# Another stored order of issue for an attention and channel-mixing kernel on one core

## The chip, the cores and the metric

The kernel runs on one NeuronCore of a Trainium2 chip; the seven other cores are idle. The metric is the device time of one execution in microseconds, and the median over several executions is compared.

## What is computed

The input is q, k and v of 8 batches and 8 heads, 1152 positions of 64 numbers each. Queries are averaged in pairs, so 576 queries per head meet 1152 keys. The result, brought to 8 batches of 576 rows of 512 numbers, goes through a gated feed-forward step whose inputs are blends of each row with the row ahead of it.

```python
q_pool = q.reshape(B, H, S // factor, factor, D).mean(axis=3)
scores = scale * np.matmul(q_pool, k.transpose(0, 1, 3, 2))
attn = np.exp(scores - max); attn = attn / (sum + 1e-09)
x = np.matmul(attn, v)          # heads side by side: (B, 576, 512)
xk = mu_k * x + (1.0 - mu_k) * x_prev
xr = mu_r * x + (1.0 - mu_r) * x_prev
k = np.maximum(xk @ w_k, 0.0)
v = k * k @ w_v
r = 1.0 / (1.0 + np.exp(-(xr @ w_r)))
return r * v
```

## The kernel before

**Attention.** There are 64 head passes, and each is cut into 6 blocks of 96 queries: 384 blocks. A block's scores are nine TensorE (PE) matmuls of 128 keys by 96 queries into one of three score buffers in PSUM, s0, s1, s2 (L512, the high parts). VectorE (DVE) takes the maximum over the nine (L534). PE turns that maximum round with an identity matrix (L537), DVE reduces it across the keys (L545), ScalarE (ACT) writes the result into a row of the query tile (L526), and nine more matmuls add the low parts and subtract the maximum at once (L517). ACT takes the exponential into pf (L559), and GpSimd (POOL) cuts the low halves out of it (L521). In the first 60 blocks the maximum goes through a matmul of its own (L549). The products with the values are done in windows of 128 queries: per key chunk the matmuls L586, L588 and L591 into the one buffer a. After the last window of a head DVE divides by the sums (L607 to L612), and the result is turned, by PE (L637) for the first batch and by DMA transposes of st (L624) and a POOL addition (L626) after that, into xt.

**Feed-forward.** Tiles of 256 rows. DVE makes the blends (L743, L733, L751), PE does all products at one line (L784: w_k with 256 columns, w_r and w_v with 512), ACT takes relu, square, tanh and exp (L811, L813, L832 to L837), POOL splits the squares (L815), DVE gates (L839, L848), and a DMA writes the rows (L851). Each matrix is stored as a high and a low part. The weights are fetched and split in the first 150 us (DMA L663, ACT L671, L675, L688, DVE L678 and L690, POOL L696).

**Loads.** Keys kr and values vr (L444) and queries qr (L409) come by DMA two passes ahead. ACT and DVE or POOL split them (L452, L457, L411, L414, L418, L476, L479, L482); DMA transposes turn keys into ks1 (L468) and queries into qT (L434), and a DMA copies ks1 into ks2 (L471). All DMAs are issued by one queue, that of SyncE (SP), which waits in order.

**The order.** Nothing is put on an engine as the Python code runs. `Issue.add` only records each operation with its engine, an assumed duration and its dependencies. `Issue.run` then reads the string TURNS: for each engine in turn (DMA, DVE, ACT, PE, POOL) a number says which of the operations still left comes next. So the string alone fixes in which order every engine, the DMA queue among them, gets its work. `Issue.follow` gives each operation an assumed start under that order, and operations are emitted by these starts. `Issue.gaps` looks at the assumed pauses of PE in the first 150 us and fills a part of them with matmuls on zeros (fillers, L914), whose results are added to nothing. These keep PE occupied.

```python
ENGINES = ("DMA", "DVE", "ACT", "PE", "POOL")
turns = iter(zlib.decompress(base64.b85decode(turns)))
for e in ENGINES:
    left = [n for n in range(len(ops)) if eng[n] == e]
    while left:
        k = 0
        while (step := next(turns)) == 255:
            k += 255
        order.append(left.pop(k + step))
```

Of the kernel before, what the change touches and what calls it, by code (L numbers as in the profile page):

```python
# [29 lines left out]
SW = 256.0  # L30
# [25 lines left out]
    "(ss#m?0^w7$<h<1X<1%TCq1caDZ?;rv`Y%l!ACdg+L-_;mSZYG2d`(Dfr#lEcnm+H8)VzMrWpo$O(lic6f%f3lqls&nHn3ZflBSAQbVcKTp3@fHdm=!p)%Fg"
    "mFkLh#d@lvd{L<{mWmz4oRXzXE|bgVaI8<~>+@8gd=|yIY$B0PB$9<>HlJ<H<r3K{N)o9=GL@u6W?nXfTdG-k7sV5?csvuIl+I*g=}bDEj>Te$SRO?!X;d6d"
    "H>N3-PDLV#NF)}C_ViJAPfxg8A<ygZytXza*h0;&+oS}j+NLzMP^DUIYN95yTyAKz3xy(_Dwm8Rm5O?OJ=NDyU7?&#=X0r4sy>YqD&zs>bS9>zwWJyjhqXuq"
    "9Z!wu>oA2w3I&7QRSvg&$g&i)Xdpo7Bd6>*x^C%aK{o<A7X)yQh6Z+YM+X`X!80aWTT?wX?1nWp;Nh&@G@X`~7UWbkZdqw;Y-m8cSE-56*5$^6nMZ5Z<?9Ol"
    "g+g9ai&=CQdzqtJJ0=tPL?V~S5T#RTHL0nZu37D_tLZ8M*9yas3a+kC)@{c|w_BDjJ%eAe042I_Ii1gsvoQoM4anC}71=8MHsN^~t_RT?0X5)a)LCk)V>LHd"  # L60
    "t5tTsv5^7OP;G$caGe@Wor;vrqSte|TyHK{QoFKhx<F{(Y$lV<Fe=z68_%%kDbybCifd|Ai>R&}!YDz@hA5Qx20Tv#hnR{1jKk>57WNw*?i+!XE*Ij3{C6Xu"
    "+m<iF-f5Z_#O4N2I9D4`C!3Q@b%Huxb=3a;CH?&d_4cYg<7n(yxZXiM-R-arn9*S<S__6od(*_Wqubglt!<T-N~O|NsnEd~BrT1qp@CJ<X$_jH0#rZ|fSb*x"
    "GgO$HD&+HdN+y%(Bp}9_+@xGCpW|^LyDycX1fexlHI>rC30()`DGHE<TqO{76$*ujyx^eXGSDzw8BvqljkY#jZ_%4|9gb8gbFsAoMXfC}TcvkR6`-fFu~}7{"
    "nsoIrOM`a}C7`DsJ%SD)%G9L?3I!z(>}OLM_6$QbnZziA&B|o_&dDbe33vyiG=^R(1@~fVG-aeTJ8p1SX#p6i0Y^bohd_WqFSsBWJPfa(kS=?}Fvc4F{d!;D"
    "(mtGZ>tn`rb#?W3QD1K_TDqrOQw>#XZ-%K=z1pOjt!2Hr*;9L~O>h}JQ|C8pp`hn-MMbTz17qcL+^XEH)XB}7%i+Zm*-S&W=6WIvoQ;FyHLu~f5s4tCcrn$a"
    "uo?=7bcI}(0cBf?hj6oq+c@B3%OAT2yUo_y*UKeix&RO4RaMtR9o!9CYb)?x(VKYe>J4V83G`W36tzTD-<s7jq@*$_kQssQ67Vp~%{l61GSS9JfT!s=tQe<Q"
    "o*Ou7L=uJrDCpoHCE$7N6}K@drePq0asnR6Z(r~W%x`RL#H0>0RD{hS;*|kX0L>dJ6aDDm*AWd##kt|?4rmGkR>4igo1)-Uk+%;_8Gy|kIDCL}Q>LP10L7Cg"
    "j-No|$0=i}U+wQxdbP0_Bwf8dy*)h>y2f{Rb#W)F7)zaMXNS_>+ScFJ*4ozEN-dLHIwo{tXtgM9Rx33%H&v0EsM=qxR%EtPQOo6VEoJ7GWz{lDnh=nx<+0VW"
    "LX|RFx75(En0a!rVOfc0&ze=7HFKt-)J><tv}y1;J1`mVFd;RGlnE2Y(YSGmcz>L_mF^yjz%8_BJ9V~_($?luOQ2Z=*H$d6vDiRXu?VE8B}E15D3{NtGg%OB"
    "5-gij6pEuq;-z>o!kKWSnZjWVP>)#Qcx=d#>jdfoj-x_kq%brT+csu^K!eO%2KUxXV+Oas!iq_OwP;jjzAuj&lS|nr)D{i~eI+W6;rCUjSgd2us2c;fUZISV"  # L70
    "CZH>gUQ3b^ZKFt}8c9c>sY0R7Pz0H<7lLc-mg{;h;-l+=SDl#S)WJms^l0*)Oq1bma0r{A%Z%QmPnAA0gEq5^RH<~r%hqyvEWE6+mjjI*lK0_Tsk=njmr4^z"
    "L2S(z3cwGru5iqj23#c+Zn|hw6rPqC@)T<g$D#^*8V+@ZlyDojDS0djov4hhwjEH&K9afIkWI*jQM=F&uJgGmHGq4PGLdNf`0?m)X%l9R<&%DpdVhaE_0df5"
    "O+QWR8-pWtc6HIru1=!%xeB#*f<38~s!CM_7^pl6FNhAP;@!&SgUiZfWQs}=dWUsSp-=}?pl%oy>2yk3mARF`luC+X7~FFbl#C}9P@J_2zc4x_Gz*08_4j*y"
    "gpoqs-Q6?0-7!kn-0rS1)TMSR9n?Ofy{(O?g{_^awY61kQJb5UGMfJYz#oI5aawr{f=@$38<l_!7}fKU>I-#EeRb?0<ypx<fc0}ElFiRP5@!>ds>Er23~r^P"
    "(PT6liLiTfBN4<K&pW{L6b4N1+}>UVE;`iJ$?eo`!Wn97X`Kn5THD|r2o!^}r3v0uX<E5U0#`O1nr)htkVSS6W2&yuz)rDiRgOE9%aHUdl>$j;%D#IFI8uqn"
    "RccH|6Le@S7H22n8;>*c!ZeQ$9)Qd+1~$kZgK#p~)um8Jhe>VSZ3L3hTP4*HRf)snMCldt2vr)(9h1sL5VfU>Y%%<Ch$*mlP*wF%vPzo!v7BmzPxZ2EnY@!k"
    "@p!$2FM9+7c#-E54^k0v8iOksz(6C3S_OkjF(uzBHHj_FA)YJ||M{k2h5@pc`B5=08A6J3Lj62IQAV1jISwW@re|`w7S=QnOEiio20@RidF+r09}NSi5cHmd"
    "X@q9-6G4<iyUOYVvMvwR7<d7Alt@^<YpUt0csLNS?Qj@xj);!;2;&Oz!{9hVH71`!hXK?M2OPYm6$n@u#HJ}d;(K`}7jvRSRx*h?Tz<r};GFcraxKs$deF8*"
    "p`@L_FTww$lkhLq-X~0Uf-eR5VaOu99@$WF(4-u@BM~Q)k-kZfLS{UUp9jNv@G^+E;?970Pk3?EfOoQkcGQjF2GklvH%9>@^6*=M5IOt^*N<5i-qYcZM#W}*"
    "ef?-7ODFg3!%=8L!^J)ONa#YRPrl$M_kQ>x_8)%o;isSO-o1D4Zrt**P-xFbAB~KBJTkIx<X<DZa2)wyWY;dDJ@hF*^f#iv@7%rn-T!&_J)*z<)yKp?-~QX*"  # L80
    "-{#C;wr$(CW5@RG+hy_J-XePE%~xc8>&q{{x)sMi(Hn0Nz4FS_Tj;45pL&X3MA_yoTYmRDdUklz@bI(4!<#oh^9(=n=u<?v;fW`Rens>cZ5SSYWW&R<vR~7q"
    "kJ3XAadzXw4{zLv;~g-%f8*^NZePEiZoBQa`yPCd?xmj-cK6}(U3cHLZk_M!9oT+CbTbVN{dnlQp|7BR<uyb<^s|>@`!3N%Yu2t^L#tP>z6jfYU2+NbbT+M#"
    "x14p>*?jocw`k?c6)RS(TuF2~&cFFhzlIa(lv9>3U&`5Kbka#*|2ol8M91N5*^(s-X~BX8#~i=lxUYRp-h4D2d+bq1&6_um=!m1}$VH0|B07)`T{O7xkV6Is"
    "al^dB52v|v{hH?xvV(&xbOsI>m@{YAEMN1`?AbGBOomOT88c|wH2?02Q>W5|2{PN+**|e&XJ4N@>B01&yPG&nRyr#^JsllPJ|IwznAAv^ILM12BYA(NQV-_K"
    "=XnPzVpR^yh>!?j{tFYf@Pro=mazEDijl+`pV!(KAjD2#K+^8dY2UujKBJF5BH-$aFFyHX7i{<EpYPrcu<a)L=+lozb_0BSMn3pN;t%#d?WFhL1Mc31{q5a<"
    "{9_b<Z|?vu-+1dSdj0jc7=?e?_WJ9iz4|h}_S&ER1em?>0&RWemCc*~@Q2Mrf8a~M|NZ98@}6ht`Qhh)HMS>f&po=~kqwV+*zgGFA0xu?m&n~u^x*nCiPkf)"
    "0HUAs<vZ7{`#CZ<aQ>(M(?1>>x^~D%*VXhNcCp;AUVZMl7hOcOibw*9&O8$kB1Y2b45V)WOJ|;W;))fteEITI=(N*LJ^@8^{3x=P0$a<LFDFJ8>{vSf_+ySa"
# [867 lines left out]
```

## Time and profile before

| | |
|---|---|
| three executions | 1104.06, 1099.98, 1105.12 us; median 1104.06 us |
| profiled execution | 1100.48 us, of it 1098.7 us from the first to the last instruction |
| busy PE, DVE, ACT, POOL | 97%, 80%, 69%, 68% of the span |
| mean granted TensorE clock | 0.998 of full speed |
| HBM | 67.11 MB read, 9.44 MB written |

A busy share counts the time in which at least one instruction of that engine runs. Matmuls overlap each other in the pipeline, so PE counts as busy also where the next matmul comes a little late; only longer pauses show as idle time. "L534" is line 534 of the kernel before; in the changed kernel every line after the table has a number larger by 2.

### The profile page before, as it was taken

Reading aid. Unit: us, or ns where it says so; the run is one execution under the profiler, and the core shown is the slowest. Engines: PE = TensorE matmul, PEld = TensorE weight load, DVE = VectorE, ACT = ScalarE, POOL = GpSimd, SP = SyncE. Lnnn points to the kernel's source line nnn. Section 1 sums busy time; section 2 is a strip of 40 time slices with the busy share of each in tenths; the row PEclk is TensorE's granted clock in tenths of the full one; section 3 lists DMA queues with packets and bytes.
Section 4 is the critical chain, followed back from the end, with each engine's and each line's share of the span. In section 5 each row is a group of like instructions: output and inputs, shape, how many; then the busy total and the mean of one; then the engine's idle time right before and its main releaser. Section 6 shows DMA issues by size and latency. Waiting matters only on the chain. (4 is left out here: it accounts for less than half of the span.)

```text
span 1098.7 us, 43186 instructions
## 1 busy us (share of the span) xinstructions
PE 1068.2 (97%) x18625; PEld 875.1 (80%) x18625; DVE 873.6 (80%) x1565; ACT 763.0 (69%) x1419; POOL 746.4 (68%) x750
## 2 busy tenths in 40 slices
...
GB/s 229 215 214 144 169 195 105 186 144 112 148 122 126 128 101 144 142 112 131 125 99 125 123 140 128 104 93 175 65 135 141 99 147 76 146 32 35 10 20 39
DMA packets 257647, 135.25 MB, mean 123 GB/s; under 512 B 192944, under 2 KB 229808, under 8 KB 257456
## 3 DMA queue, kind: packets, MB, share of 16 engines
...
q8 instruction: 145, 2.38, 0.9%
...
HBM read 67.11 MB, written 9.44 MB: 70 GB/s over the span
## 5 line engine op out<-in xcount | busy, mean ns | idle before, releaser
L521 POOL TENSOR_SCALAR pl<-pf 128x864 f16<-128x864 uint16 (+1 forms) x384 | 353.7, 921 | 190.5 <-ACT pf L559 157.9
L534 DVE TENSOR_REDUCE mx<-s 128x96 f16<-128x864 f32 x384 | 402.4, 1052 | 57.1 <-PE s L512 39.8
L559 ACT ACTIVATE pf<-s 128x864 int32<-128x864 f32 x384 | 339.9, 888 | 137.1 <-PE s L517 110.4
L586 PE MATMUL a<-vt,pf 128*128 128x65 f16 x2880 | 302.0, 193 | 4.2 <-issue 2.7
L588 PE MATMUL a<-vt,pf 128*128 128x64 f16 x2880 | 302.3, 193 | 0.0
L586 PEld LDWEIGHTS <-pf 128*128 128x128 f16 x2880 | 255.4, 98 | 9.2 <-issue 2.8
L588 PEld LDWEIGHTS <-pf 128*128 128x128 f16 x2880 | 250.5, 98 | 15.2 <-issue 2.5
L591 PE MATMUL a<-vb,pl 128*128 128x65 f16 x2304 | 254.2, 193 | 0.0
L512 PE MATMUL s<-qT,ks 128*128 128x96 f16 x3456 | 225.7, 206 | 4.2 <-ACT pf L559 2.5
L517 PE MATMUL s<-qT,ks 128*128 128x96 f16 x3456 | 223.3, 206 | 1.9 <-ACT qT L526 1.5
L591 PEld LDWEIGHTS <-pl 128*128 128x128 f16 x2304 | 212.8, 97 | 0.1
L512 PEld LDWEIGHTS <-ks 128*128 128x128 f16 x3456 | 186.6, 98 | 30.5 <-issue 5.9
L517 PEld LDWEIGHTS <-ks 128*128 128x128 f16 x3456 | 181.2, 98 | 21.8 <-issue 2.9
L526 ACT ACTIVATE qT<-s 1x96 f16<-1x96 f32 x384 | 90.4, 236 | 98.6 <-PE s L537 80.7
L545 DVE TENSOR_REDUCE mx<-s 128x1 f16<-128x128 f32 x324 | 92.9, 287 | 66.0 <-ACT qT L526 64.0
L784 PE MATMUL f<-xhk,wk_hi 128*128 128x256 f16 x496 | 135.1, 272 | 0.9 <-DVE em L848 0.7
L784 PE MATMUL f<-xlk,wk_hi 128*128 128x256 f16 x496 | 135.1, 272 | 0.2 <-DVE xlk L751 0.2
L784 PE MATMUL f<-xhk,wk_lo 128*128 128x256 f16 x496 | 135.2, 273 | 0.0
L784 PEld LDWEIGHTS <-wk_hi 128*128 128x128 f16 x1152 | 105.8, 98 | 15.1 <-issue 1.3
L815 POOL TENSOR_TENSOR gl<-g 128x512 f16<-128x512 f32 x72 | 79.0, 1104 | 39.7 <-ACT g L813 25.9
L537 PE MATMUL s<-identb,mx 128*128 128x128 f16 x384 | 84.5, 221 | 8.9 <-DVE mx L534 5.6
L784 PE MATMUL f<-wv_hi,g 128*128 128x512 f16 x240 | 90.9, 379 | 1.2 <-ACT ex L832 1.2
...
## 6 DMA issues: line engine op xcount, KB each, us to landing
...
out_dram<-em SPq DMA_DIRECT2D x36, 256.0 KB, 2.9
...
```

Source lines behind the costliest of these rows:

```text
L512: nc.tensor.matmul(cols(c, c + 1), ks1[hp][:, c, :], qhi, start=(c == c0), stop=False, skip_group_check=True)
L517: nc.tensor.matmul(cols(c, c + 1), ks2[hp][:, c, :], qlo, start=False, stop=True, skip_group_check=True)
L521: op("POOL", 0.917 if buf == ("pside",) else NC * (r1 - r0) / 1200 + 0.27, lambda: nc.gpsimd.tensor_scalar(to, half(pf, U16, 0)[:, :, HALF ...
L526: op("ACT", 0.131, lambda: nc.scalar.activation(qlo[0:1], src, AF.Prelu, scale=scale, alpha=(1.0 + EPS) / (1.0 - EPS)), r=[("s", at)] + kl ...
L534: op("DVE", 0.974, lambda: nc.vector.tensor_reduce(mxz[:, P - QN:P], grid(0, NC).rearrange("p c q -> p q c"), axis=AX.X, op=ALU.max), r=[( ...
L537: op("PE", 0.057, lambda: nc.tensor.matmul(s[:, 0:P], mxz, identb, start=False, stop=False, skip_group_check=True), r=[("mx", z), ("col", ...
L545: op("DVE", 0.199, lambda: nc.vector.tensor_reduce(to, s[:, 0:P], axis=AX.X, op=ALU.max), r=[("s", z), ("row", z)], w=[("col", z1) if join ...
L559: op("ACT", NC * QN / 1200 + 0.067, lambda: nc.scalar.activation(pf[:, :, HALF + rows.start:HALF + rows.stop], grid(0, NC), AF.Exp, bias=S ...
L586: nc.tensor.matmul(a_b[:, a0:a0 + VN], half(pf, F16, 1)[:, c, his], vt[jv][:, c, D:D + VN], start=(w == 0 and c == 0), stop=False, skip_gr ...
L588: nc.tensor.matmul(a_b[:, a0:a0 + D], half(pf, F16, 1)[:, c, his], vt[jv][:, c, 0:D], start=False, stop=(side and c == NC - 1), skip_group ...
L591: nc.tensor.matmul(a_b[:, a0:a0 + VN], pl[:, c, rows], vb[jv][:, c, 0:VN], start=False, stop=(c == NC - 1), skip_group_check=True)
L784: nc.tensor.matmul(ps, terms[i][0], terms[i][1], start=(first and i == 0), stop=(i == last), skip_group_check=True)
```

## The change

Only the string TURNS is another one, two lines longer. No operation of the kernel, no tile, no size and no dependency differs. The new string is said to come from a search that judges an order over several draws in which transfers land late or early; the old one was found with one fixed lateness. Since the fillers follow from the assumed pauses, their number changes too: 146 before, 168 now.

```diff
 TURNS = (
-    "c-nnh378bswLZ01b#?W=ch7XsbWhJd%*H-|AjpUUE`SSB&>$KmZV`mIJQs{Hnm9(IQAsrJ8YODLBrb8HPesKTh*8`yQ4?MgM{q$=3HSZyR*&Y(_r7=TRMo9p"
...
-    "T?^f<*o`LtM-!o+jgpC)(PD~RtBi#5=+IDvYKxWOP!V3o6kbvZan%a>EBTINhS0SZn}fGk%s{|2ZNsrGn-qggUDf6C<(HuLmpDe(H2xQVP3K+"
+    "c-n1x378ed+3wrR={|i<pM9CL%$eoPzA+07>#ztSOHd#nzZ>I-CSpWHL`6l>ENV1H{+JjSaES)=YGOiAqwzPRCYlJwl?08(M8{k;Dx)Ic+V}mc58mfK&#ju%"
...
+    ">(u"
 )
```

The following rows show three places. In names such as qT0 or ks1_0 the number behind the tile is the buffer; the number after the underscore only counts tiles. First, the SP queue (all DMAs) at the head of the program, before:

```order
L434 DMA_TRANSPOSE qT0_85<-qn0_69 128x4x128
L444 DMA vr0_75<-in_v_dram 128x576
L434 DMA_TRANSPOSE qT0_85<-qn0_69 128x4x128
L663 DMA st1_122<-in_moe_w_k_dram 128x1024
L471 DMA ks2_1_84<-ks1_1_82 64x1152
L663 DMA xt2_107<-in_moe_w_k_dram 128x1024 x2
L434 DMA_TRANSPOSE qT1_86<-qn0_69 128x9x128
L663 DMA st0_121<-in_moe_w_k_dram 128x1024
L434 DMA_TRANSPOSE qT1_86<-qn0_69 128x9x128
L468 DMA_TRANSPOSE ks1_0_81<-kn0_79 128x9x128
```

and now:

```order
L436 DMA_TRANSPOSE qT0_85<-qn0_69 128x4x128 x2
L665 DMA st1_122<-in_moe_w_k_dram 128x1024
L473 DMA ks2_1_84<-ks1_1_82 64x1152
L665 DMA xt2_107<-in_moe_w_k_dram 128x1024 x2
L470 DMA_TRANSPOSE ks1_0_81<-kn0_79 128x9x128
L446 DMA vr0_75<-in_v_dram 128x576
L665 DMA st0_121<-in_moe_w_k_dram 128x1024
L384 DMA mu_r_156<-in_moe_mu_r_dram 128x4x1
L436 DMA_TRANSPOSE qT1_86<-qn0_69 128x9x128
L665 DMA st1_122<-in_moe_w_k_dram 128x1024
L436 DMA_TRANSPOSE qT1_86<-qn0_69 128x9x128
```

The transpose of the third head's keys (ks1_0) moved ahead of the two transposes of the next queries (qT1); the third head's values (vr0) moved behind three fetches of weights.

Second, DVE at the head of the program, around the first maxima, before:

```order
L466 COPY ks1_0_81<-s0_131 128x512
L411 TENSOR_TENSOR qs0_78<-qr0_77 128x256
L479 SCALAR_TENSOR_TENSOR vt0_87<-vr0_75,vt0_87 128x4x64
L534 TENSOR_REDUCE mx0_96<-s0_131 128x96
L534 TENSOR_REDUCE mx1_97<-s1_132 128x96
L545 TENSOR_REDUCE mb0_99<-s0_131 128x1
L479 SCALAR_TENSOR_TENSOR vt0_87<-vr0_75,vt0_87 128x5x64
```

and now:

```order
L413 TENSOR_TENSOR qs0_78<-qr0_77 128x256
L468 COPY ks1_0_81<-s0_131 128x512
L459 TENSOR_TENSOR kn1_80<-kr1_74,kn1_80 128x9x64
L536 TENSOR_REDUCE mx0_96<-s0_131 128x96
L536 TENSOR_REDUCE mx1_97<-s1_132 128x96
L547 TENSOR_REDUCE mb0_99<-s0_131 128x1
L481 SCALAR_TENSOR_TENSOR vt0_87<-vr0_75,vt0_87 128x4x64
```

Between the copy of ks1 and the first maximum, two steps (qs and a part of vt0) gave way to one (the low part of the second head's keys, kn1); the vt0 step now stands behind the first L545.

Third, DVE around block 198, in the middle of the run, before:

```order
L534 TENSOR_REDUCE mx2_98<-s2_133 128x96
L733 SCALAR_TENSOR_TENSOR xk_108<-xr_109,mu_k_155,xt2_107 128x192
L839 SCALAR_TENSOR_TENSOR ex0_117<-ex0_117,em0_119 128x512
L545 TENSOR_REDUCE mx0_96<-s2_133 128x1
L534 TENSOR_REDUCE mx0_96<-s0_131 128x96
L733 SCALAR_TENSOR_TENSOR xk_108<-xr_109,mu_k_155,xt2_107 128x192
```

and now:

```order
L536 TENSOR_REDUCE mx2_98<-s2_133 128x96
L735 SCALAR_TENSOR_TENSOR xk_108<-xr_109,mu_k_155,xt2_107 128x192
L547 TENSOR_REDUCE mx0_96<-s2_133 128x1
L536 TENSOR_REDUCE mx0_96<-s0_131 128x96
L735 SCALAR_TENSOR_TENSOR xk_108<-xr_109,mu_k_155,xt2_107 128x192
L841 SCALAR_TENSOR_TENSOR ex0_117<-ex0_117,em0_119 128x512
```

The gate step of the feed-forward (L839, now L841) moved from ahead of a maximum to behind it.

## Rows read from the trace of the kernel before

**Rows 1.** The page: busy time by engine, and the instruction packets of PE's queue.

```profile
PE 1068.2 (97%) x18625; PEld 875.1 (80%) x18625; DVE 873.6 (80%) x1565; ACT 763.0 (69%) x1419; POOL 746.4 (68%) x750
...
q8 instruction: 145, 2.38, 0.9%
```

**Rows 2.** Busy time by stretch; columns: length, engines with counts, clock, DMA share, GB/s.

```profile
0.00:10.00 10.00, 7.36 (x95) 7.00 (x95) 7.21 (x29) 6.45 (x12) 3.36 (x11) 1.00 0.78 229
10.00:50.00 40.00, 33.24 (x677) 29.52 (x675) 34.91 (x64) 30.78 (x60) 17.11 (x20) 0.96 1.09 243
50.00:150.00 100.00, 94.12 (x2030) 84.77 (x2027) 96.73 (x169) 88.16 (x171) 72.22 (x73) 1.00 0.81 179
150.00:1000.00 850.00, 840.27 (x15164) 695.98 (x15163) 701.82 (x1240) 601.67 (x1117) 629.23 (x626) 1.00 0.59 121
1000.00:1098.70 98.70, 93.19 (x669) 57.78 (x667) 32.94 (x66) 35.90 (x64) 24.46 (x23) 1.00 0.10 26
```

**Rows 3.** Waits of PE, 150 to 1000 us: us in total, times, longest.

```profile
PE s L537 <- DVE mx L534: 4.0, 11, 1.0
PE s L537 <- DVE mx L545: 2.8, 7, 0.7
PE a L586 <- DVE xb L612: 1.1, 2, 0.7
```

**Rows 4.** Waits of PE and then of DVE, start of the run to 150 us.

```profile
PE a L586 <- issue: 2.7, 1, 2.7
...
DVE mb L545 <- PE s L537: 3.7, 2, 3.4
```

**Rows 5.** DVE in order of time, 8 to 10 us.

```profile
8.37 0.42 DVE L411 TENSOR_TENSOR qs<-qr 128x256 f32<-128x256 f32 x1
8.71 0.92 DVE L479 SCALAR_TENSOR_TENSOR vt<-vr,vt 128x256 f16<-128x256 f32 x1
9.54 2.01 DVE L534 TENSOR_REDUCE mx<-s 128x96 f16<-128x864 f32 x2
```

**Rows 6.** The fillers by line: count, busy us, mean ns of one, idle us before them.

```profile
L914 PE MATMUL a<-zero 128*128 128x128 f16 x83 | 8.6, 265 | 0.9 <-DVE zero L329 0.9
...
L914 PE MATMUL s<-zero 128*128 128x128 f16 x63 | 5.1, 221 | 0.0
```

**Rows 7.** PE in order of time, around 24 us.

```profile
23.79 0.20 PE L591 MATMUL a<-vb,pl 128*128 128x65 f16 x1
26.71 0.24 PE L586 MATMUL a<-vt,pf 128*128 128x65 f16 x1 [2.72 <-issue]
```

**Rows 8.** DMA packets by queue, 11 to 24 us, and 24 to 31 us below.

```profile
q1 hardware_dynamic: 4036, 3.31, 100.4%
q14 instruction: 1, 0.01, 0.2%
...
q8 instruction: 2, 0.03, 2.0%
```

**Rows 9.** The SP queue, then POOL, in order of time, 14 to 33 us.

```profile
14.53 0.51 SPq L444 DMA_DIRECT2D vr<-in_v_dram  x1
...
23.01 1.70 SPq L434 DMA_TRANSPOSE qT<-qn  x1
...
27.36 2.51 SPq L468 DMA_TRANSPOSE ks<-kn  x1
...
23.50 0.67 POOL L482 TENSOR_SCALAR vb<-vr 128x576 f16<-128x576 f32 x1
32.13 1.42 POOL L521 TENSOR_SCALAR pl<-pf 128x864 f16<-128x864 uint16 x2 [7.96 <-issue]
```

**Rows 10.** DVE, POOL and PE in order of time, 496 to 500 us.

```profile
497.07 1.38 DVE L839 SCALAR_TENSOR_TENSOR ex<-ex,em 128x512 f32<-128x512 f32 x1
498.38 0.28 DVE L545 TENSOR_REDUCE mx<-s 128x1 f16<-128x128 f32 x1
498.58 1.04 DVE L534 TENSOR_REDUCE mx<-s 128x96 f16<-128x864 f32 x1
...
496.03 1.89 POOL L521 TENSOR_SCALAR pl<-pf 128x864 f16<-128x864 uint16 x2 [1.36 <-ACT pf L559]
...
499.68 0.23 PE L537 MATMUL s<-identb,mx 128*128 128x128 f16 x1 [1.02 <-DVE mx L534]
```

**Rows 11.** Two DVE lines: duration in ns, min/median/max.

```profile
L839 DVE SCALAR_TENSOR_TENSOR ex<-ex,em x36: 674/693/1384, 164.1 to 1093.8; 128x512 f32<-128x512 f32 x36
...
L733 DVE SCALAR_TENSOR_TENSOR xr<-xr,mu_r,xt x96: 269/477/1661, 134.1 to 1066.5; 128x256 f32<-128x256 f32 x48, 128x64 f32<-128x64 f32 x16, 128x192 f32<-128x192 f32 x16, 128x128 f32<-128x128 f32 x16
```

**Rows 12.** The chain that ended last, its pieces off PE after 1000 us.

```profile
1010.98 0.18 SPq L851
...
1011.27 4.37 DMA st<-st
...
1094.86 0.69 DVE em L848
```

More of the change, by code (lines that the diff above doesn't have):

```diff
@@ L56 @@
[L56 to L87, printed above, removed]
@@ new lines @@
+    "(=*|!uukbiIue?lgOy7L-B2)O1#R20+;lt?3p!4)6hp`kXvi6Cj|KwJLq^uo<DrlfEb4kp<O;`v!64#xD1bydV1`mb%d%~&1imAs4p@=6WtfJOMIsms1$8$b"
+    "v~?@trh>s#F2q}TV>%e%I|SplX=Q_MFbl&r?0^B&NJpd8O@`0l$<~7j7r~Gnv%|4~MfI6ciz*HT_yCI&sO!`NG)|XB{b-y>qp_(`YiQ85`ufiL`f@$$8Yeb4"
+    "Hlw+zp%D!zm+F~oODLgOtJT!j)uINuTuUyOFEH2TP*tocq8i0~L1RNYU6oE}sx$dwzO7J5=bPD*&ZaZj4AQxy)LqSa>6J=lQt5O)Jtddtc==qisw$aGrjx}~"
+    "F4bCvT%xK9_1SDymiS6CCwkG>)7y)lD3R6~iL|$CZYx^C;U+DF=60>AwF%9&O(6>1P+u;UtZI}3g<@@eEo#l0+8UHfRg|(^EM}Ri_(H4|Q9xBrPZ*hu8H?$O"
@@ new lines @@
+    "s2Pb;ML^6c#RyQ>jkva*vJoU=Y*=B0D#>&lLd6V(@+^lO$4UAPRC35PIBCSx0?X2M-8FQgR}boTm(%5T*lcUj^`^!~k<_5tQP+$nO>|wZuCC!<X+o(KFp9-M"
+    "T_Imnqn8Ygau!giPv@x2X`;$}Do40xh=Y`2Seg-~1X@so9kgpHXCM%Q<4j~@MJOIv45}nzn`X5%srrd*BCez(1jaUOJ)lbpha(XRFVfq38(LdiS~RUmBV5dK"
+    "S+B2euBYTpgpwYp18VYSE?3Cq^Z9~-s!~-46`Uy+nhMBso(YR|COxH)My?8+R^2dDrfJ9Zcq|;&-4Gu`3$((8a99gXL`Cv|BvH2Gh?0Hj<z1>OHQQDVaEujH"
+    "x=q8e^cW3McO$xCI7b;%?E!s?%)<nIyx!kG)ZcH68)u?#0>+Q0<XwH}?PTgQI=ecJjt)a-TMIhS-q^;(S!!%<>g4fjjX+Cli{2d2DOSB+uh&8=X($%5Dxss0"
@@ new lines @@
+    ";j7Q3Rb(J9s}kX!&-YU!L_Dn^odyKydNymAx{*w#=)1z<STt;f5_(9SC^2V+!?VL-dMi2#YoOCQp+jp&dmCS~$!zpfTYKA_b{<+=Dc=x*MDVnhb)%`t(d}~C"
+    "Fzf2{LZMVD=y??K8mg+bVsTPY<|CiU&>ESDqMV<7S*K>ww9FhWnhDt~%`ufs>WOS1lhO4$%St8;U9j(ld7_aJE3WG<jkutvR|YXpX3R9lN|I^m={~NzdrbG3"
+    "F@1gL>qT!*Zx3~?cXa3h3a<w&!_pgC4Wp%5uhSc9%e8t<Z7pF?UENS!trzQ{8K9MB3Wf2-!ni^~#HOk<1*KQYpUWL49w(C)T#4jaB{vhLC5)pfJ(+|SkJIbX"
+    "mNi=?8fVyA77mMl*Fp{|sHzCwH@460?KREu-R2mev$wBT@9EJ^nz7-unXLptLqkKL+)ze+v#vEZa%gnb)tPm*rco+UB%)ssQC%%|oAX5#FPQ1zixfn~QbkP)"
```

92 lines of the change are left out of this document (57 added, 35 removed).

## Prediction

> **What bounds the kernel now.** I read the page first. PE is busy for 1068.2 of 1098.7 us, DVE for 873.6 [rows 1], so at most 30.5 us of the span show PE idle, and a mere reordering can win no more than that plus what little hides between matmuls. Next I cut the span into stages [rows 2], because the share of busy time mixes three of them.
>
> In the first 10 us PE idles for 2.64 us: data are not there yet. From 10 to 50 us PE idles for 6.76 us and from 50 to 150 us for 5.88 us, but there DVE is the bound: it works for 34.91 of 40 and 96.73 of 100 us, since it also splits the weights. What the start can give back is therefore DVE's own idle time, 5.09 and 3.27 us, together 8.4 us. From 150 to 1000 us PE idles for 9.73 us of 850, DVE for 148: PE bounds, and the waits that are left are short ones for the maxima, 4.0 us in 11 waits for L534 and 2.8 us in 7 for L545, and 1.1 us in 2 for the division of the sums [rows 3]. After 1000 us PE idles for 5.51 us. Part of that is the end: the last gate starts at 1094.86 us, and then the result is written [rows 12]; nothing in an order shortens it.
>
> So the visible stakes are 8.4 us in the start, 9.7 us in the middle, and little at the end.
>
> **The change, part by part.** All operations stay, with the fillers as the only ones that are added. Outside the three places shown, the table moves hundreds of steps by one or two places; I price the stages.
>
> *First maxima.* In the trace the first L534 starts at 9.54 us, behind the 0.92 us of a vt0 step that began at 8.71 us [rows 5]. Now that step stands behind the first L545, and the low part of kn1 stands in the place of qs and vt0. At worst this brings nothing, since the scores themselves have to be there; at best the first maximum comes 0.83 us earlier (9.54 less 8.71). I take 0.3 us, nearer to nothing: the moved step is still DVE work, and DVE is full right afterwards. Term: -0.3 us.
>
> *Fillers.* 22 more, at 94 ns each (8.6 and 5.1 us for 146 of them [rows 6]), are 2.1 us of PE time. They stand in the first 150 us, where PE has 15.3 us of idle time by the stages above and DVE sets the pace. They are hidden by that; if the cover were gone they would cost the whole 2.1 us. Term: +0.3 us.
>
> *The DMA queue in the start.* At 23.79 us PE stops for 2.72 us, and the releaser named is "issue": nothing that the trace shows held it [rows 7]. DVE then waits 3.4 us for PE, its only long wait from 10 to 150 us (two waits of this kind, 3.7 us together) [rows 4]. From 11 to 24 us the data queue has 100.4% of the engines' time and not one packet of PE's instruction queue is seen; two come in the 7 us after [rows 8], where 145 over 1098.7 us [rows 1] would make about one per 7.6 us. So I read the stop as PE out of instructions behind a crowded set of DMA engines. The Trainium skill (Runtime: NRT & Kernel Launch, Instruction fetch mechanics) says that instructions come in 16 KiB blocks by a DMA queue of the engine's own and that crossing a block's end is mostly hidden; by that rule the stop would be an accident, the new order would not have it, and the sum would be lower by 2.7 us. The rows show 2.72 us that were not hidden, so the sum goes by the rows. The new order keeps the crowd: three fetches of weights still stand one behind another there, and one transpose moves from 27.36 us to ahead of the one issued at 23.01 us [rows 9]. The stop may go (-3.4 us, DVE's wait) or come twice (+3.4 us). Between these ends I take 0, as the queue before and now holds the same transfers within a few places. The values vr0, moved behind three fetches, were issued at 14.53 us and used by POOL at 23.50 us, after which POOL stood idle for 7.96 us [rows 9]. That idle time hides a lateness of some microseconds, so I price it at nothing; without it POOL's next cuts, and the windows behind them, would wait as long as the values do, which lies inside the 3.4 us if they come by 27 us.
>
> *The middle.* Here DVE is often full only for a moment. At 497.07 us the gate L839 takes 1.38 us where its median is 0.693 us, then L545 and L534 follow, and PE waits 1.02 us at L537 [rows 10, 11]. It is a slow copy of L839 and not its place alone: until 497.92 us POOL was cutting low halves (two L521 from 496.03 us, 1.89 us together [rows 10]). In the new order L839 stands behind that maximum, so this wait should go. But the other orders of steps meet other POOL steps. To judge this I counted, for blocks 60 to 383 and with the median durations of the trace, the DVE work between two successive maxima against the PE work between the ends of their scores: DVE has more by over 0.5 us in 15 places before and in 8 now, and over all places where it has more, the excess is 19.3 us before and 17.3 us now. Ten per cent less excess on 9.73 us is 1.0 us. The ends are -9.7 us (every visible wait goes) and +9.7 us (as many again). Term: -1.0 us, close to nothing, because the count hardly moves.
>
> *The end.* One output DMA stood between two transposes of the last result, on the chain for 0.18 us [rows 12]; now it stands ahead of both. Against it, ACT now does both scalings of the last mix ahead of a tanh and an exp, which then wait for the transposes. I take 0, ends -0.2 and +0.6 us.
>
> Sum: -0.3 + 0.3 + 0 - 1.0 + 0 = -1.0 us. Against the profiled execution's own 1100.48 us that is 1099.5 us. That execution lies 3.6 us below the median of the three runs (1104.06 us), near the lowest (1099.98 us); the mean of the four is 1102.4 us. Less 1.0 us this gives 1101.4 us, and **1101 us** is my forecast.
>
> **The rivals.**
>
> *Faster.* The start loses its stop and the middle half of its waits: 3.4 + 0.5 x 9.7 = 8.3 us, thus 1102.4 - 8.3 = 1094 us. For it: the place of the wait of 1.02 us is visibly relaxed, 15 crowded places became 8, and an order that was judged against late and early transfers should depend less on one. Against it: the waits of PE in the middle name DVE and no DMA [rows 3], so what such a search guards against is not what costs time there.
>
> *Slower.* DVE steps with two inputs in SBUF fall under POOL steps more often. The place is DVE's queue from 150 to 1000 us; the price is what L733 shows, 1661 ns against 477 ns, or L839 with 1384 against 693 [rows 11]; it decides once such a step stands directly ahead of a maximum about twice as often as now. Then the visible waits double: 1102.4 + 9.7 = 1112 us. For it: hundreds of small moves draw these meetings anew, and nothing in the string knows where POOL really is. Against it: the count of crowded places did not rise. The Trainium skill (SBUF — State Buffer, Who interferes with whom) has the rule: DVE and GpSimd share one pair of ports under an exclusive lock, and the loser blocks until the other's instruction ends. The 1.38 us beside POOL's 1.89 us agree with it [rows 10].
>
> *The order changes nothing that ends last.* The fillers and the table move, but each stage is bound as before: 1102.4 us. This lies in the forecast's own range.
>
> **How the numbers follow.** About 0.5% (5.5 us of 1104.06) is what a measurement of this kernel can tell from no change; that puts "faster" below 1098.5 us and "slower" above 1109.6 us. The forecast with the case of no effect has 0.48, the faster rival 0.34, the slower one 0.18. I lean to the faster side because both counts that I could make fell. The forecast's own range, by the stop (3.4 us either way) and some of the middle, is 1097 to 1106 us. To leave out no more than 2 in 10 it has to reach towards both rivals: 1091 us takes in the faster one, 1110 us the slower one up to its last part.
>
> **What would show it.** Right: the stages 150 to 1000 us still show 8 to 11 us of PE idle time, mostly L537 waiting for DVE; DVE stays above 95% busy from 50 to 150 us; a stop of PE with releaser "issue" of 2 to 4 us somewhere before 60 us; 168 fillers, without a longer start. The wait at block 198 should be gone. The forecast is wrong if PE idles for less than 6 or more than 15 us in the middle, if DVE's idle time from 10 to 150 us leaves the band from 5 to 12 us, or if PE waits for a DMA anywhere after 150 us.

## The result and the profile after

Before: 1103.68 us, the median of four executions (1099.98 to 1105.12). After: 1090.78 us, the median of four (1087.42 to 1091.95). The ratio is 0.9883, with a 95% interval from 0.9849 to 0.9917: **faster by 12.9 us**, and 0.2 us below the low end of the predicted range. The profiled execution of the changed kernel took 1087.42 us, of it 1085.6 us from the first to the last instruction, against 1098.7 us in the one before, so 13.1 us less.

The page of the changed kernel, answering to [rows 1]:

```profile
PE 1064.7 (98%) x18647; PEld 876.1 (81%) x18647; DVE 865.6 (80%) x1565; ACT 761.7 (70%) x1419; POOL 745.3 (69%) x750
...
q8 instruction: 146, 2.39, 0.9%
```

DVE does the same 1565 instructions in 8.0 us less. Busy time by stretch, with the columns of [rows 2]:

```profile
0.00:10.00 10.00, 7.99 (x80) 7.49 (x81) 5.99 (x28) 6.15 (x11) 2.48 (x10) 1.00 0.74 223
10.00:50.00 40.00, 35.07 (x765) 31.31 (x762) 38.18 (x68) 32.75 (x64) 19.51 (x22) 1.00 1.06 231
50.00:150.00 100.00, 94.42 (x2036) 85.55 (x2033) 96.11 (x171) 88.58 (x173) 72.10 (x73) 1.00 0.81 190
150.00:1000.00 850.00, 845.54 (x15260) 700.96 (x15259) 694.47 (x1248) 604.05 (x1119) 630.26 (x627) 1.00 0.58 121
1000.00:1085.60 85.60, 81.70 (x521) 50.79 (x519) 30.89 (x54) 30.19 (x55) 20.93 (x19) 1.00 0.06 23
```

From 150 to 1000 us PE's idle time fell from 9.73 to 4.46 us. Waits of PE there, answering to [rows 3]:

```profile
PE s L539 <- DVE mx L536: 2.3, 4, 1.0
PE f L786 <- ACT ex L834: 1.2, 1, 1.2
PE s L539 <- DVE mx L547: 0.3, 1, 0.3
```

The waits for the two maxima went from 6.8 us in 18 to 2.6 us in 5. No wait for a DMA is among them. The single wait for ACT is near 997 us; the kernel before has one just like it after 1000 us, outside its stretch.

**Where in time the 13.1 us come from.** Each block has one L537 (now L539), so the same block can be found in both traces. Block 59 starts its L537 at 137.11 us before and 136.42 us after, 0.7 us earlier. From block 59 to block 383 it takes 861.1 us before and 850.3 us after, 10.8 us less; from there to the end 100.5 and 98.9 us, 1.6 us less. But PE does its matmuls in another order, so the same block is not the same amount of work done. The feed-forward products ahead of block 59's turn, before and now:

```profile
0.00:137.11 137.11, 9.77 (x72) 6.45 (x72) 0.99 0.89 194
0.00:136.42 136.42, 11.61 (x84) 7.36 (x84) 1.00 0.90 203
```

The new order has by then done 12 more of these, 9 more L512 and 5 more L517 (now L514 and L519), 1.9 us of work at the median distances of 0.109 and 0.042 us from one such matmul to the next; ahead of block 383 it has done 0.9 us more. Counted by equal work PE has gained 2.6 us by block 59, **9.9 us in the middle** and 0.7 us at the end. All differences of the middle below are counted in this way; from block to block each is 1.0 us larger.

**Idle time shows only half of it.** From 150 to 1000 us PE has 5.27 us less idle time, yet the middle is 9.9 us shorter. A matmul counts as busy to its modelled end, while the next could start much earlier (L591 and L586 follow each other at some 0.03 us and each is shown for 0.2 us). I measured each distance from one matmul's start to the next against the median distance for its kind. By that sum PE lost 18.1 us from 150 to 1000 us before and 9.9 us after. Of it 11.6 us in 31 places before, and 5.6 us in 20 after, stand directly ahead of L537, the matmul that waits for the maximum.

**What the new order does on DVE.** Its two-input steps are shorter on average. Lines of DVE from 150 to 1000 us in the kernel before (count, busy us, mean ns, idle us ahead):

```profile
L479 DVE SCALAR_TENSOR_TENSOR vt<-vr,vt 128x576 f16<-128x576 f32 x54 | 49.2, 911 | 0.4 <-ACT vt L476 0.4
L411 DVE TENSOR_TENSOR qs<-qr 128x576 f32<-128x576 f32 x26 | 26.7, 1028 | 0.0
L751 DVE SCALAR_TENSOR_TENSOR xlk<-xk,xhk 128x512 f16<-128x512 f32 x28 | 25.4, 910 | 0.9 <-ACT xhk L748 0.8
```

and in the changed kernel:

```profile
L481 DVE SCALAR_TENSOR_TENSOR vt<-vr,vt 128x576 f16<-128x576 f32 x53 | 53.1, 1003 | 0.0
L413 DVE TENSOR_TENSOR qs<-qr 128x576 f32<-128x576 f32 x26 | 24.2, 930 | 0.1
L753 DVE SCALAR_TENSOR_TENSOR xlk<-xk,xhk 128x512 f16<-128x512 f32 x29 | 20.3, 703 | 0.9 <-ACT xhk L750 0.7
```

The low parts xlk take 703 instead of 910 ns each, qs 930 instead of 1028; the values vt go the other way, 1003 instead of 911. I call **stretch** what DVE's steps take beyond the lower quartile of their own line and shape. Over 150 to 1000 us it is 51 us before and 42 us after. And in the run of DVE steps that leads up to a late maximum, the stretch is as long as the loss in 11.1 of the 11.6 us before, and in 5.0 of the 5.6 us after. Each of the 92 steps that took over 0.15 us more than their quartile before (84 after) ran while a POOL step ran. POOL runs most of the time and such a run of steps can be long, so this shows that the stretch is enough, not that it is the cause. So theory 1 was: PE waits for maxima that are late because, just ahead of them, DVE's steps stood still beside POOL's. Theory 2: DVE's work is spread better between maxima, POOL or no POOL. Theory 3: transfers.

The place around block 198 [rows 10], DVE in the changed kernel in order of time:

```profile
489.63 0.29 DVE L547 TENSOR_REDUCE mx<-s 128x1 f16<-128x128 f32 x1 [0.33 <-ACT qT L528]
489.88 1.06 DVE L536 TENSOR_REDUCE mx<-s 128x96 f16<-128x864 f32 x1
490.85 0.41 DVE L735 SCALAR_TENSOR_TENSOR xk<-xr,mu_k,xt 128x192 f32<-128x192 f32 x1
491.19 0.68 DVE L841 SCALAR_TENSOR_TENSOR ex<-ex,em 128x512 f32<-128x512 f32 x1
```

and POOL there:

```profile
486.98 4.09 POOL L523 TENSOR_SCALAR pl<-pf 128x288 f16<-128x288 uint16 x4
491.57 1.07 POOL L523 TENSOR_SCALAR pl<-pf 128x864 f16<-128x864 uint16 x1 [0.50 <-ACT pf L561]
```

The gate L841 now runs behind the maximum and begins in a gap of POOL (491.07 to 491.57 us): 0.68 us where it was 1.38 us. The wait of 1.02 us is gone.

### The profile page after: what moved, and what is told of

Read it like the earlier page. It is cut to its first block, busy times and chain, and to the rows that moved or that the text cites. A ratio compares the mean times of both kernels' runs of the same rounds, so it can differ in the third digit from the quotient of the medians.

```text
span 1085.6 us, 43226 instructions
## 1 busy us (share of the span) xinstructions
PE 1064.7 (98%) x18647; PEld 876.1 (81%) x18647; DVE 865.6 (80%) x1565; ACT 761.7 (70%) x1419; POOL 745.3 (69%) x750
## 4 chain that ended last, share of the span: by engine, by line
PE 89%; DVE 6%; ACT 2%; issue 1%; DMA 0%; ACTq 0%; DVEq 0%
PE f L786 35%; PE s L514 12%; PE s L519 12%; PE a L588 7%; PE a L590 7%; PE a L593 6%; PE s L786 5%; DVE mx L536 3%; PE s L539 2%; PE a L786 2%; ACT pf L561 1%; DVE xr L735 0%; PE s L551 0%; DVE mx L547 0%; DVE xb L614 0%
## 5 line engine op out<-in xcount | busy, mean ns | idle before, releaser
L590 PE MATMUL a<-vt,pf 128*128 128x64 f16 x2880 | 309.4, 193 | 1.4 <-issue 1.4
L588 PE MATMUL a<-vt,pf 128*128 128x65 f16 x2880 | 309.1, 193 | 0.7 <-DVE xb L614 0.3
L593 PE MATMUL a<-vb,pl 128*128 128x65 f16 x2304 | 258.3, 193 | 0.0
L514 PE MATMUL s<-qT,ks 128*128 128x96 f16 x3456 | 232.1, 206 | 4.1 <-ACT pf L561 3.4
L519 PE MATMUL s<-qT,ks 128*128 128x96 f16 x3456 | 230.5, 206 | 1.5 <-ACT qT L528 1.2
L514 PEld LDWEIGHTS <-ks 128*128 128x128 f16 x3456 | 189.6, 98 | 34.2 <-issue 6.9
L519 PEld LDWEIGHTS <-ks 128*128 128x128 f16 x3456 | 184.0, 98 | 20.4 <-issue 2.2
L786 PE MATMUL f<-wv_hi,gl 128*128 128x512 f16 x240 | 91.0, 379 | 0.0
```

Source lines behind the costliest of these rows:

```text
L514: nc.tensor.matmul(cols(c, c + 1), ks1[hp][:, c, :], qhi, start=(c == c0), stop=False, skip_group_check=True)
L519: nc.tensor.matmul(cols(c, c + 1), ks2[hp][:, c, :], qlo, start=False, stop=True, skip_group_check=True)
L588: nc.tensor.matmul(a_b[:, a0:a0 + VN], half(pf, F16, 1)[:, c, his], vt[jv][:, c, D:D + VN], start=(w == 0 and c == 0), stop=False, skip_gr ...
L590: nc.tensor.matmul(a_b[:, a0:a0 + D], half(pf, F16, 1)[:, c, his], vt[jv][:, c, 0:D], start=False, stop=(side and c == NC - 1), skip_group ...
L593: nc.tensor.matmul(a_b[:, a0:a0 + VN], pl[:, c, rows], vb[jv][:, c, 0:VN], start=False, stop=(c == NC - 1), skip_group_check=True)
L786: nc.tensor.matmul(ps, terms[i][0], terms[i][1], start=(first and i == 0), stop=(i == last), skip_group_check=True)
```

## The experiments

**One half of the order at a time.** Both strings in one kernel; every step that one order assumes to start before 150 us stands in that order, all others follow in the other.

```diff
+        first = plan(new)
+        q = {e: [n for n in new[e] if first[n] < 150.0] + [n for n in old[e] if first[n] >= 150.0] for e in ENGINES}
```

New start, old rest:

> The new order up to 150 us of its own assumed starts (on every engine and the DMA queue), the old order for all steps after that. Between the two full orders the difference is 12.9 us; by the block times in the traces about 3 us of it had come by 150 us and about 10 us came between 150 and 850 us. If the stages add up, this kernel wins the start's part alone: 1100 to 1101 us, and PE idles some 9 to 10 us from 150 to 1000 us, as before. If a better start is what makes the middle better (steps of POOL and DVE meet elsewhere because they begin elsewhere), it comes near the changed kernel, 1091 to 1095 us. If the start's part was chance, 1103 to 1105 us.

Old start, new rest (the same with the two swapped):

> The old order up to 150 us of its own assumed starts, the new order for all steps after that. If the stages add up: 1093 to 1095 us (1090.8 plus about 3), and PE idles 4 to 6 us from 150 to 1000 us. If the middle's gain hangs on the start, 1099 to 1104 us. The sum of this kernel's gain and the other hybrid's should be near 12.9 us if the parts are independent.

Measured: 1101.19 us (ratio 0.998, 0.9963 to 0.9997) and 1094.84 us (0.9915, 0.9891 to 0.994), 2.2 and 8.5 us below the kernel before; together 10.7 of 12.9 us, the rest within the intervals. PE's line for 150 to 1000 us, new start with old rest:

```profile
150.00:1000.00 850.00, 837.91 (x15108) 693.79 (x15107) 701.36 (x1235) 598.78 (x1110) 623.02 (x623) 1.00 0.59 120
```

and old start with new rest:

```profile
150.00:1000.00 850.00, 843.96 (x15250) 700.13 (x15249) 695.82 (x1239) 604.83 (x1119) 628.04 (x628) 1.00 0.60 121
```

The stages add up: about a sixth of the gain comes with the start, two thirds with the rest, whose idle time follows the new order (6.0 us) and not the new start (12.1 us).

**POOL's cut of the low halves shortened**, in both orders. The later blocks read stale low halves.

```diff
-  to, half(pf, U16, 0)[:, :, HALF + r0:HALF + r1], LO, ...
+  to[:, 0:1] if i >= 60 else to, half(pf, U16, 0)[:, 0:1 if i >= 60 else NC, HALF + r0:HALF + r1], LO, ...
```

> The old order with POOL's cut of the low halves (L521) shortened from nine key chunks to one from block 60 on, so that the low halves of the later blocks are not renewed: POOL is busy for far less, and DVE steps with two inputs in SBUF meet hardly any POOL step. Theory 1 (the middle's gain is fewer and shorter DVE steps that stand still beside a POOL step): the stretch of the DVE steps, 51 us in the trace of the kernel before from 150 to 1000 us, nearly goes, and this kernel falls by 8 to 14 us, to 1090 to 1095 us. Theory 2 (the gain is DVE work that is spread better between the maxima, by the order alone): it falls by less than 5 us, to 1099 to 1103 us. Theory 3 (transfers that come late): no change but what the cut itself held, within 3 us.

> The new order with the same shortening of POOL's cut from block 60 on. Read against the old order with the same shortening: theory 1 says the difference falls from 12.9 us to about 3 to 6 us (the start's 3 us and a rest); theory 2 and theory 3 say that it stays at 10 to 15 us. Absolutely: theory 1 gives 1085 to 1089 us, theory 2 1086 to 1090 us; the difference between the two orders decides, not this number.

Measured: 1096.97 us (0.9941, 0.9921 to 0.9961) and 1088.05 us (0.9858, 0.9832 to 0.9885). The old order fell by 6.4 us, the new one by 2.7 us; the difference shrank from 12.9 to 8.9 us. Both numbers lie between the theories. POOL was still busy for 402 us and DVE's stretch still 28 and 26 us.

**All repeated POOL steps shortened**, in both orders; keys, values, blends and squares of the middle are then stale in part as well.

```diff
-  gl[:, f2, 0:n], g32[:, f2, 0:n], gh[:, f2, 0:n]
+  gl[:, f2, 0:n // 8 if t0 else n], g32[:, f2, 0:n // 8 if t0 else n], gh[:, f2, 0:n // 8 if t0 else n]
...
```

> The old order with all of POOL's repeated steps shortened to about an eighth or less (L521 from block 60, the low parts of keys L457 and the values L482 from pass 12, L623 and L626 from the third and fifth batch, L763 and L815 from the second tile on); the skipped parts keep stale numbers. Shortening L521 alone took 6.4 us off the old order and 2.8 us off the new one, and left POOL busy for 403 us from 150 to 1000 us and DVE's stretch at 28 and 26 us. Theory 1 (meetings with POOL steps are the whole of the middle's difference): a further fall of 4 to 6 us, to 1091 to 1093 us. Theory 1 and 2 together (about half each): 1 to 3 us lower, 1094 to 1096 us. Theory 2 alone: within 1 us of 1097.

> The new order with the same shortening of all POOL steps. What decides is the difference to the old order with the same shortening, 8.9 us when only L521 was short. Theory 1: it falls to 3 to 5 us (the start's part). Both theories in halves: it stays at 6 to 9 us. Theory 2: 9 us or more. Absolutely 1086 to 1088 us by all of them.

Measured: 1090.28 us (0.9875, 0.9852 to 0.9898) and 1085.59 us (0.9836, 0.9814 to 0.9858), 4.7 us apart, and 0.7 and 0.4 us below the ranges. From block 59 to 383 the two take 848.8 and 847.9 us; by equal work they do not differ (0.1 us the other way), where the full kernels differ by 9.9. The stretch of 150 to 1000 us, old order:

```profile
150.00:1000.00 850.00, 846.39 (x15308) 703.09 (x15307) 664.87 (x1255) 605.93 (x1125) 217.15 (x629) 1.00 0.59 121
```

and new order:

```profile
150.00:1000.00 850.00, 846.81 (x15275) 702.70 (x15274) 666.69 (x1257) 603.79 (x1119) 215.66 (x627) 1.00 0.59 121
```

DVE's work takes 37 us less than in [rows 2] though none of its steps changed. With POOL nearly out of the way the old order is in the middle as good as the new one. The 4.7 us are theory 1's number, and theory 2 alone falls. But shorter POOL steps also give their results earlier, and that remained as another reading.

**POOL busy again, with steps on a scrap tile.** Behind each shortened step a contiguous POOL step on a tile that nobody reads.

```diff
+  def idle(size):
+      if size > 0:
+          nc.gpsimd.tensor_scalar(junk[:, 0:size], junk[:, 0:size].bitcast(U16), LO, 1.0, ...)
```

> The old order with all POOL steps shortened as in the two kernels that shortened them all (old order 1090.3 us, new order 1085.6 us, 4.7 us apart), and behind each shortened step a POOL step on a scrap tile that nobody reads, sized so that POOL is again busy for some 630 us from 150 to 1000 us. The results of POOL are thus early, while POOL occupies itself about as long as in the full kernel. If DVE is held by POOL being at work (meetings), the gain of the shortening goes again: 1097 to 1104 us. If what counted were POOL's results coming earlier, it stays at 1090 to 1093 us.

> The new order with the same shortened POOL steps and the same scrap steps. Meetings: 1087 to 1092 us, and 8 to 13 us below the old order in the same form. Early results: 1085 to 1087 us, and 4 to 6 us below it.

Measured: 1090.65 us (0.9889, 0.9858 to 0.992) and 1084.56 us (0.9824, 0.9803 to 0.9844), so both as without the scrap steps. Read by its expectation this would speak for early results. But its condition, POOL busy for some 630 us again, failed; old order:

```profile
150.00:1000.00 850.00, 846.58 (x15309) 702.53 (x15306) 676.61 (x1252) 605.76 (x1125) 541.85 (x1159) 1.00 0.60 121
```

POOL gained 325 us of work, and DVE's busy time only 12 us. Steps of this form, in shorter pieces, hardly hold DVE, so the run says nothing on what the real steps do.

**The same with the rest of each real step**, short step first, the rest (same operands) on a scrap tile:

> The old order with POOL's steps shortened as before, but behind each short step now stands the rest of the real step (same operands, same form, about eight ninths of the length) with its result on a scrap tile that nobody waits for. The contiguous scrap steps of the last try did not occupy DVE as the real ones do: they put POOL's busy time from 217 back to 542 us, but DVE's from 665 only to 677 us, against 702 us in the full kernel. Here DVE's busy time from 150 to 1000 us should come back to 690 to 702 us. If holding DVE (and POOL's own occupation) is what costs, the old order comes back to 1097 to 1103 us. If the early results of POOL were the gain, it stays at 1089 to 1092 us.

> The new order in the same form. Meetings with POOL's real steps: 1087 to 1091 us, and 8 to 13 us below the old order in this form. Early results: 1084 to 1087 us, and 4 to 6 us below it.

Measured: 1134.13 us (1.0265, 1.0239 to 1.0291) and 1126.66 us (1.0205, 1.0183 to 1.0227), slower than anything expected. Two steps for one overfilled POOL; waits of PE from 150 to 1000 us in the old order:

```profile
PE a L605 <- POOL pl L529: 18.3, 22, 1.7
PE a L600 <- POOL pf L529: 3.3, 4, 1.2
```

POOL itself became what PE waits for, which it is nowhere in [rows 3], and DVE's 687 us stay short of the 690 to 702 us that were the condition. Inconclusive.

**Each real POOL step whole, one for one, its result on a scrap tile.** Nobody waits for POOL's results in the middle any more; what POOL does and how long stays.

```diff
-  to, half(pf, U16, 0)[:, :, HALF + r0:HALF + r1], LO, ...
+  scrap(NC, r1 - r0) if i >= 72 else to, half(pf, U16, 0)[:, :, HALF + r0:HALF + r1], LO, ...
...
```

> The old order with every POOL step of the middle (from block 72, pass 14, the third batch, the fifth batch or the third tile on, as the buffers allow) in its full length and form, but with its result on a scrap tile, so that nobody waits for POOL and the stale numbers are read. POOL's busy time from 150 to 1000 us stays near 630 us, and it is one step in the place of one step, so POOL is not overfilled as in the last pair. If DVE being held by POOL's steps is what costs: as the full kernel, 1099 to 1104 us, with PE's losses at L537 near 11 us. If POOL's results coming late is what costs: 1089 to 1093 us.

> The new order in the same form. Meetings: 1088 to 1092 us, so 9 to 13 us below the old order in this form. Late results: 1084 to 1087 us, and 4 to 6 us below it.

Measured: 1099.84 us (0.9983, 0.9968 to 0.9998) and 1091.54 us (0.9912, 0.9895 to 0.9928), 8.3 us apart. The old order by stretch:

```profile
150.00:1000.00 850.00, 840.55 (x15175) 696.68 (x15174) 704.09 (x1240) 602.13 (x1118) 615.16 (x626) 1.00 0.59 121
```

and its waits of PE there:

```profile
PE s L541 <- DVE mx L538: 3.1, 8, 1.1
PE s L541 <- DVE mx L549: 2.8, 7, 1.2
```

DVE is back at 704 us, the waits for the maxima are back at 5.9 us, and PE loses 9.9 us ahead of the matmul that turns the maximum (11.6 in the kernel before). They are the same places: of the 30 blocks at which PE lost over 0.05 us there before, 24 are late again and hold nearly all of the loss; with the POOL steps shortened 9 were left, with 1.5 us. The results of POOL, early or late, are worth some 1.8 us (0.2 to 3.5 by the interval), by which this kernel lies below the one before. What costs the old order its time is POOL being at work while DVE is: the ratio is 0.9983 with the steps whole and unread, 0.9875 with them shortened.

For the difference between the orders the pair is less clean. Its 8.3 us lie below the 9 to 13 us expected for meetings and above the 4 to 6 us for late results, and in the middle 6.4 of the 9.9 us stand. The new order in this form, by stretch and in its waits of PE:

```profile
150.00:1000.00 850.00, 844.82 (x15254) 700.76 (x15253) 698.80 (x1244) 602.12 (x1116) 612.60 (x626) 1.00 0.59 121
PE s L543 <- DVE mx L540: 3.3, 4, 1.3
```

It loses 7.2 us ahead of the turn where the changed kernel loses 5.6, of it 1.4 us at one place near 890 us where the changed kernel is not late. There two blends of DVE take 2.23 us beside POOL's addition, whose result is on scrap, and DVE is behind until the maximum:

```profile
885.80 2.23 DVE L741 SCALAR_TENSOR_TENSOR xk<-xr,mu_k,xt 128x128 f32<-128x128 f32 x2
885.68 1.22 POOL L633 TENSOR_TENSOR lw<-st 128x512 f32<-128x512 f16 x1 [0.20 <-ACT qT L532]
```

So meetings are drawn anew in this form too. That this is all of the missing 3.5 us is not shown.

**DVE's feed-forward steps cut to a few columns**, in both orders, from the second tile on:

```diff
-  xm[w][:, c, o0:o0 + ln], xm["r"][:, c, o0:o0 + ln], ..., x[:, c, s0:s0 + ln],
+  xm[w][:, c, o0:o0 + (8 if t0 else ln)], xm["r"][:, c, o0:o0 + (8 if t0 else ln)], ..., x[:, c, s0:s0 + (8 if t0 else ln)],
...
```

> The old order with DVE's five feed-forward steps (L733, L743, L751, L839, L848) cut to 8 or 16 columns from the second tile of 256 rows on; the rest keeps stale numbers. POOL, ACT, PE and all DMAs do what they did. If the middle's loss is DVE work that comes too thick between two maxima (by place, by POOL or both), nearly all of the 18 to 20 us between matmuls after 150 us goes, and this kernel comes to 1084 to 1090 us. If transfers or ACT hold the middle (theory 3), it stays above 1097 us.

> The new order with DVE's feed-forward steps cut in the same way. If DVE's lateness is the whole of the middle's difference, the two orders differ by the start's 2 to 4 us alone: 1081 to 1087 us, against 12.9 us without the cut. If it is not DVE, the difference stays above 8 us.

Measured: 1094.35 us (0.9913, 0.9886 to 0.994) and 1083.29 us (0.9822, 0.9793 to 0.9851). The new order did as expected; the old one stayed 4 us above its range, and the difference at 11.1 us, which by its expectation (above 8 us) would say that DVE's lateness is not the cause. But a large part of it is the start: in these two profiles block 59 comes at 140.6 and 135.7 us. The middle's difference fell from 9.9 to 5.4 us. Waits of PE in the old order, 150 to 1000 us:

```profile
PE s L537 <- DVE mx L534: 1.8, 5, 0.6
PE s L537 <- DVE mx L545: 1.0, 3, 0.6
```

Still for maxima: L479 (mean 935 ns) and L411 (1019 ns) were not cut and take as long as before (911 and 1028). So it is not the amount of DVE work alone: 78 us of it were taken away, and a good half of the difference stayed. The steps that were cut are themselves steps that meet POOL, so this pair does not part amount from meetings.

**The first eight weight fetches cut to an eighth**, old order; the rest of their buffers is set to zero by ACT:

```diff
+  nf = 64 if nw <= EARLY else 512
+  nc.sync.dma_start(s3[:, 0:nf], src[:, 0:nf])
```

> The old order with the first eight fetches of weights (L663) cut to an eighth of their bytes; the rest of the four buffers is set to zero by ACT where the fetch stands, so the weights are wrong. It asks what makes PE's stop named issue near 24 us: 2.7, 2.1 and 0.8 us in three profiles of the old start, 1.4, 0.8 and 1.0 us in three of the new one. Theory A (instructions come late behind a crowd of transfers): DMA share from 10 to 30 us falls well under 0.9, and the stop is under 0.4 us or gone. Rival B (the stop hangs on the program and not on the transfers): still 0.8 us or more near 24 us. In time: A gives 1098 to 1102 us, since up to 3 us come back; B 1101 to 1105 us.

Measured: 1101.23 us (0.9977, 0.9964 to 0.9989). The stop named "issue" is gone, with the DMA share at 0.25:

```profile
20.00:30.00 10.00, 7.82 (x196) 7.40 (x196) 7.87 (x13) 9.31 (x17) 3.70 (x4) 1.00 0.25 51
```

The kernel before, in the same stretch and in a part of it:

```profile
20.00:30.00 10.00, 7.28 (x169) 7.16 (x166) 6.27 (x12) 6.67 (x12) 3.58 (x4) 0.83 1.09 240
27.00:29.00 2.00, 2.00 (x38) 2.00 (x36) 0.00 (x0) 0.84 (x3) 0.00 (x0) 0.50 0.97 267
```

The clock of 0.83 is a mean over both levels: full speed (2.4 GHz), and half of it (1.2 GHz) in a part behind the stop, as from 27 to 29 us. With the fetches cut the time is in theory A's range, there is no stop, and the granted clock stays at 1.00; PE's instruction queue has two packets from 11 to 24 us, where [rows 8] show none. That PE lacked instructions is inferred from this. In place of the stop PE waited 1.2 and 0.9 us for L526 (ACT, which does the zeroing), so not all came back.

**Fewer fillers**, new order: 147 in place of 168.

```diff
-    def gaps(self, start, until=150.0, cold=8.0, share=0.6, dense=0.62, span=3.4):
+    def gaps(self, start, until=150.0, cold=8.0, share=0.49, dense=0.62, span=3.4):
```

> The new order with 147 fillers instead of 168 (a smaller share of the assumed pauses is filled), about as many as the old order has. My term for the 22 extra fillers was +0.3 us, hidden under DVE. If that holds: 1090 to 1091.5 us, no difference that can be measured. Rival: the extra fillers are part of the start's gain, since they keep PE occupied: the granted clock from 20 to 60 us falls below 1.00 in some slice, and the time is 1092.5 to 1094 us. If they cost their full 2.1 us: 1088 to 1089 us.

Measured: 1089.39 us (0.9875, 0.9856 to 0.9893), no difference from the changed kernel (0.9883) that can be told, and the clock is 1.00 in every 10 us from 10 to 60 us. So the extra fillers are not what holds the clock. Whether they cost nothing or up to 2.1 us the time does not tell: it lies between the two ranges. One thing was not expected: with as crowded a DMA (share 1.15 from 20 to 30 us) the stop near 24 us is not there, but one at 38.79 us is:

```profile
38.79 0.19 PE L590 MATMUL a<-vt,pf 128*128 128x64 f16 x1 [1.02 <-issue]
```

In this one profile, then, it is not the crowd alone that sets where PE stops.

## Why the prediction was wrong, point by point

- **The middle: this step failed.** The prediction took "-1.0 us, close to nothing, because the count hardly moves"; measured 9.9 us by equal work, and 8.5 us by the run with the old start and the new rest. Two errors are in it. First, the count was made with the median durations of the trace. That leaves out what makes a maximum late in the old order: a DVE step that takes twice as long beside a POOL step. With POOL's steps shortened the two orders do not differ in the middle; with POOL's steps whole and their results unread 6.4 us of the difference are back. The other figure, places with too much work from 15 to 8, came nearer: the places of loss went from 31 to 20, the loss to a half. Second, the stake was priced by visible idle time, 9.73 us, where by starts of matmuls 18.1 us were lost. The "what little hides between matmuls" of its first paragraph was thus some 8 us in this stretch. So with about half of the loss gone (18.1 to 9.9 us) the middle gained as much as the far end of the term, "every visible wait goes" (-9.7 us).
- **The rival "faster" had the mechanism's size almost right and its price wrong.** "The middle half of its waits" is what happened to idle time (9.73 to 4.46 us), but half the waits were worth twice as much. The start did not lose its stop.
- **The rival "slower" had the right mechanism** (DVE steps under POOL steps, at 1384 against 693 ns) **and the wrong sign.** Fewer meetings ahead of a maximum, not more. The rule cited for it (the Trainium skill, SBUF — State Buffer, Who interferes with whom) agrees with the runs for the real steps: with POOL's steps whole DVE is busy for 704 us, with them shortened for 665 us, their results read by nobody or stale in both. The contiguous scrap steps, which held DVE for 12 us in 325, agree with it less.
- **The start.** Taken as 0 with ends of 3.4 us. The hybrid with the new start gained 2.2 us (0.3 to 4.1). By the mean of eight profiles each (the kernels here that change nothing before block 60) block 59 comes at 138.4 us with the old start (136.5 to 140.6) and at 136.6 us with the new one (135.7 to 137.6); with the 1.9 us of work that the new start is ahead, that is **3.7 us gained**, at the far end of the term. In the two full kernels it is 2.6 us, and DVE's idle time from 10 to 150 us fell by as much, from 8.4 to 5.7 us.
- **The stop.** All sixteen profiles have it near 24 us, 0.8 to 2.7 us with the old start and 0.8 to 1.5 us with the new one; five of the old ones have a second, of 1.1 to 2.5 us, near 55 us. With the old start each of the eight shows a granted clock under 1.00 in some 10 us before 60 us, down to 0.83; with the new one none does. In five of the eight the clock falls within 1.3 us of the end of a stop near 24 us, in the other three elsewhere. That the weight fetches have a part in the stop is shown; the Trainium skill (Runtime: NRT & Kernel Launch, Instruction fetch mechanics) has the fetch of instructions as mostly hidden. If the stop is such a fetch, it was not hidden here, in sixteen profiles of sixteen. How much of the start's gain is the shorter stop or the clock, and how much DVE's order, was not tried.
- **First maxima**, -0.3 us: nothing that can be told. The first L534 starts at 9.8 us on the mean of the eight profiles with the old start (9.54 to 10.10) and at 9.7 us with the new one (9.18 to 9.88). **Fillers**, +0.3 us: nothing that can be measured; there are 168:

```profile
L916 PE MATMUL s<-zero x104: 218/221/223, 11.0 to 115.5; 128*128 128x128 f16 x104
L916 PE MATMUL a<-zero x64: 218/312/314, 0.9 to 71.8; 128*128 128x128 f16 x64
```

- **The end**, taken as 0: from block 383 on the new rest takes 98.4 to 98.9 us in every profile, the old one 99.3 to 100.6 us. But 0.9 us of that is work that the new order has done ahead of block 383; by equal work 0.7 us is left between the two full kernels, and nothing in four of the six other pairs. Before, PE waited 0.5 us there for xlk, now not.
- **The signs.** DVE's idle time from 10 to 150 us is 5.7 us, in its band; DVE is 96% busy from 50 to 150 us; no wait for a DMA after 150 us; the wait at block 198 is gone. The stop is 1.4 us, not 2 to 4:

```profile
26.57 0.20 PE L590 MATMUL a<-vt,pf 128*128 128x64 f16 x1 [1.44 <-issue]
```

  And PE idles 4.46 us in the middle, under the 6 us that were named as proof of a wrong forecast.

What stays open: the 3.5 us of the middle that did not come back with POOL's steps whole, and why this order meets POOL less ahead of maxima. The runs show fewer and smaller losses there, not that judging orders by late and early transfers brought it about; in the middle no wait for a transfer went, since there was none.
